# Rotary attention with a spatially gated MLP on one Trainium2 core: the first loads in whole rows, four idle matmuls, and the last store in halves

## The chip, the cores and the metric

The kernel runs on one core of one Trainium2 chip. A core has a matrix engine (TensorE, PE in the profile; its weight loads are listed apart as PEld), a vector engine (VectorE, DVE), a scalar engine (ScalarE, ACT), GpSimd (POOL) and SyncE (SP), which here issues every DMA. [...] The metric is the device time of one execution in microseconds (us), as the median of the runs taken. The profile calls the time between the first and the last instruction the span.

## The reference

Eight batches, eight heads, 576 positions, 64 values per head. Queries and keys are rotated by their position, softmax attention is computed per head, and its output goes through an MLP with a gate that mixes positions:

```python
q_rot, k_rot = rotate(q), rotate(k)              # x1*cos - x2*sin, x1*sin + x2*cos
scores = matmul(q_rot, k_rot.T) / sqrt(64)
attn = exp(scores - max) / (sum(...) + 1e-09)
x = matmul(attn, v)                              # heads side by side: 8 x 576 x 512
h = maximum(x @ w_in, 0);  u, v = halves of h    # 512 wide each
v_n = (v - mean(v)) / sqrt(var(v) + 1e-06)
v_s = einsum('ts,bsd->btd', w_spatial, v_n) + b_spatial[None, :, None]
out = (u * v_s) @ w_out                          # float32, 8 x 576 x 512
```

## The kernel before, in words

Two heads form a pair; there are 32 pairs, four to a batch. For each pair the kernel loads q and k, transposed and laid out as rows of 2 x 576 values (each value, and beside it the partner that the rotation needs), and v. The rotation multiplies a row by a table of cosines and sines (`tabs`) and adds the two halves. For q the table also carries the factor 1/8 (`tabq`, a scaled copy that ACT makes once). Scores are computed in tiles of 128 queries by 576 keys (`sc`, two PSUM buffers): PE multiplies, DVE takes the maximum of each row (`nmx`), ACT takes the exponential (`e`) and sums it. The exponentials are transposed on PE (`tp`), copied out of PSUM (`et` or `eh`) and multiplied by v (`pv`). For the first three pairs q and k are used as plain float32; for the later ones each operand is split into a rounded and a remaining part. The weights of the MLP arrive as 64-bit words and are decoded on DVE and ACT into float32 (`decode`: per 128x512 piece six DVE steps, tiles `dcwi`, `sgwi`, `wi`, `dcwo`, `wo`); this work lies beside the first pairs. Four pairs make a batch; then its MLP runs (`pa` first product and normalisation, `pb` the other half, `pc` mixing of positions, `pd` output), beside the attention of the next batch.

The order on every engine is written out by a small list scheduler at build time (`Program.run`, lines 138 to 220). Each operation is given an engine, an assumed duration, a key, and the names that it reads and writes. The scheduler plays the program through with these assumptions; where an engine is free it takes the ready operation with the lowest key, if a buffer for its result is free. DVE and POOL operations marked `port` are kept apart. On the chip each engine then runs its list strictly in order and waits by semaphores for what it needs. Changing the first operations therefore changes the lists later on as well.

The change touches the work at the very start. In `prepare_whole` (lines 446 to 483) the case `i == 0` handles pair 0: k and the table are loaded in two halves each, alternating (lines 464 and 465), then q (466). DVE multiplies each half of k by its half of the table (469), adds the halves into `kf` (458, 459), multiplies q by the table in two pieces of 192 and 384 columns (473), and adds (474). With `kf` and the first piece of q the first score tile can start (548). In the profile q and k are both named `st`. POOL fills constants in `setup` (290 to 298), first of all the 128x128 identity matrix `ident`, which the transposes use. At the other end, `mlp` stores each output tile `ob` (128x576) with one DMA (806) once ACT has filled both halves (805).

Of the kernel before, what the change touches and what calls it, by code (L numbers as in the profile page):

```python
# [14 lines left out]
ALU = mybir.AluOpType  # L15
AX = mybir.AxisListType
P = 128
# [206 lines left out]
def tile_attention_gated_mlp(  # L224
# [63 lines left out]
        nc.gpsimd.memset(ap.bitcast(F32), value)  # L288

    def setup():  # L290
        make_identity(nc, ident)
        nc.gpsimd.memset(bias, -896.0 * 2**23)
        for t in sums:
            nc.gpsimd.memset(t, 1.0)
        fill(qs[0][:, S:], 0.0)
        fill(qs[1][:, :TW], 0.0)
        fill(qz[64:P, :S], 0.0)
        fill(qz[0:64, S:], 0.0)
# [7 lines left out]
    def load(dst, src):  # L306
        nc.sync.dma_start(out=dst, in_=src)
# [138 lines left out]
    def prepare_whole(i, b, hp, key):  # L446
# [12 lines left out]
            e.tensor_tensor(out=kf[:, :TW], in0=k[:, 4 * P:S], in1=k[:, S + 4 * P:], op=ALU.add)  # L459

        if i == 0:
            for part in range(2):
                cols = slice(S * part, S * part + S)
                op(DMA, 820, -70 + part, lambda part=part, cols=cols: load(k[:, cols], qk[b, hp, 1, :, part]), w=[(k, part)], new=[] if part else [k])
                op(DMA, 820, -70 + part, lambda part=part, cols=cols: load(tabs[:, cols], tab[:, part]), w=[("tabs", part)])
            op(DMA, 1640, -68, lambda: load(q.tile, qk[b, hp, 0].rearrange("p c n -> p (c n)")), w=[q], new=[q])
            op(ACT, 1053, -50, lambda: nc.scalar.activation(tabq, tabs, AF.Copy, scale=0.125), r=[("tabs", 0), ("tabs", 1)], w=["tabq", "tabs"])
            for part in range(2):
                op(DVE, 680, -60, lambda part=part: nc.vector.tensor_tensor(out=turn(k, part, slice(0, S)), in0=turn(k, part, slice(0, S)), in1=turn(tabs, part, slice(0, S)), op=ALU.mult), r=[("tabs", part)], w=[(k, part)], port=True)
            op(DVE, 830, -59, lambda: sum_k(nc.vector), r=[(k, 0), (k, 1)], w=[kf], new=[kf], port=True)  # L470
            for n, (c0, c1) in enumerate(((0, Q0), (Q0, S))):
                cols = slice(c0, c1)
                op(DVE, dve_ns(2 * (c1 - c0)), -58 + 2 * n, lambda cols=cols: nc.vector.scalar_tensor_tensor(out=c2(q.tile)[:, :, cols], in0=c2(q.tile)[:, :, cols], scalar=0.125, in1=c2(tabs)[:, :, cols], op0=ALU.mult, op1=ALU.mult), r=[q, ("tabs", 0), ("tabs", 1)], w=[(q, n)], port=True)
                op(DVE, dve_ns(c1 - c0), -57 + 2 * n, lambda cols=cols: nc.vector.tensor_tensor(out=turn(q, 0, cols), in0=turn(q, 0, cols), in1=turn(q, 1, cols), op=ALU.add), w=[(q, n)], port=True)
# [242 lines left out]
    def mlp(b):  # L717
# [75 lines left out]
        for m in range(4):  # L793
            ob = Buf("m", [P, S], F32, f"ob{b}_{m}")
            for c in range(2):
                pm = Buf(pm_pools, None, None, f"pd{b}_{m}{c}")
                c0 = c * HALF
                for d in range(4):
                    def mul(d=d, m=m, c0=c0, pm=pm):
                        for n, (i, j) in enumerate(((0, 0), (0, 1), (1, 0))):  # L800
                            at = c0 + j * S
                            nc.tensor.matmul(pm[:, :HALF], lhsT=wout[d,][:, i, m * P:(m + 1) * P], rhs=gs[d][:, at:at + HALF], start=(d == 0 and n == 0), stop=(d == 3 and n == 2))  # L802

                    key = mm(3 * pe_ns(HALF), mul, r=[f"wo{d}", (gs[d], 0, c), (gs[d], 1, c)], w=[pm], new=[pm] if d == 0 else [])
                op(ACT, act_ns(HALF), key + K_OB, lambda ob=ob, pm=pm, c0=c0: nc.scalar.activation(ob[:, c0:c0 + HALF], pm[:, :HALF], AF.Copy), r=[pm, *[(ob, 0)][:c]], w=[(ob, c)], new=[ob] if c == 0 else [])
            op(DMA, 800, key + K_OUT, lambda m=m, ob=ob: load(out[b, m * P:(m + 1) * P, :], ob.tile), r=[(ob, 0), (ob, 1)])

    def norm(b, t, pm, key, sum_halves):
# [39 lines left out]

    pairs = [(b, hp) for b in range(B) for hp in range(NP)]
    prepped, xs, chain = [], [], []  # L850
    op(POOL, 800, -26, setup, w=["ident", "bias", ("sums", 0, 0), ("sums", 1, 0), ("qz", 0), ("qz", 1), ("qs", 0, 0), ("qs", 1, 0)])
    prepare(0)
    for c in range(4):
        decode(DEC_V[c], win, (1, c), w_in[c * P:(c + 1) * P, 2 * HF:4 * HF])
# [81 lines left out]
```

## Time and profile before

| what | value |
| --- | --- |
| runs of the kernel before | 967.85, 968.44, 974.62 us; median 968.44 |
| profiled execution | 968.03 us, of which the span is 966.3 us |
| PE busy | 940.3 us, 97% of the span |
| DVE, ACT, POOL busy | 667.7, 734.7, 572.3 us |
| first matmul | 11.04 us after the start of the span |

The views used are the table of busy time by stretch (each engine's busy time in a window, with its number of instructions), the chain of waits (the work that ended last, followed back), the timeline (instructions in order, with the idle time of the engine before them in brackets), the rows of one tile or line (duration of one: smallest, median, largest), the DMA view of a window, and the list of waits. A matmul of float32 operands appears as two instructions in the profile. Neighbouring instructions on an engine can overlap a little, so the distance from one start to the next is at times shorter than a duration.

### The profile page before, as it was taken

The numbers are of one execution on the slowest core, as the hardware profiler recorded it, in microseconds if no ns is written. First come the engines' busy times: TensorE is split into PE (matmuls) and PEld (weight loads), VectorE is DVE, ScalarE is ACT, GpSimd is POOL, SyncE is SP. The second block draws the span as 40 slices with busy tenths as digits, with TensorE's granted clock in tenths as the row PEclk, the third lists the DMA queues.
The fourth block names the chain that finished last, engine by engine and source line by source line (L and its number), as shares of the span: only waits on it lengthen the run. The fifth ranks groups of instructions, "written<-read, shape, count | busy, mean of one in ns | idle before, by whom it ended". The sixth has DMA issues, their size and how long they took to land.

```text
span 966.3 us, 19411 instructions
## 1 busy us (share of the span) xinstructions
PE 940.3 (97%) x6618; PEld 853.8 (88%) x6618; DVE 667.7 (69%) x1484; ACT 734.7 (76%) x1828; POOL 572.3 (59%) x501
## 2 busy tenths in 40 slices
PE   3999999999999999999999999999999999999998
PEld 2455689999899999999899998999889998999998
DVE  5899887766867667666776658676686766866331
ACT  3778788777987779777897779877798678976452
POOL 5851446566757757775666766666586765672121
PEclk9999999999999999999999999999999999999999
DMA  7671743445343553446444444445524455430101
GB/s 280 210 233 27 208 130 109 127 119 152 104 138 110 165 152 84 119 116 180 124 131 114 123 150 124 126 122 151 145 76 130 126 166 145 108 83 13 63 1 50
DMA packets 54581, 121.56 MB, mean 126 GB/s; under 512 B 12881, under 2 KB 12881, under 8 KB 54482
## 3 DMA queue, kind: packets, MB, share of 16 engines
q1 hardware_dynamic: 54482, 120.32, 44.0%
q8 instruction: 53, 0.87, 0.4%
q14 instruction: 46, 0.38, 0.1%
HBM read 66.03 MB, written 9.58 MB: 78 GB/s over the span
## 4 chain that ended last, share of the span: by engine, by line
PE 77%; ACT 9%; DVE 8%; DMA 3%; issue 2%; POOL 0%; SPq 0%; ACTq 0%; DVEq 0%
PE sc L538 12%; PE pc L787 12%; PE pv L602 11%; PE tp L578 11%; PE pd L802 10%; PE pb L769 9%; PE pa L746 5%; ACT e L561 3%; PE sc L548 3%; DVE nmx L559 2%; PE pv L675 2%; ACT eh L589 2%; ACT vv L829 2%; DVE el L313 1%; PE tp L637 1%
## 5 line engine op out<-in xcount | busy, mean ns | idle before, releaser
L589 ACT ACTIVATE eh<-tp 128x384 fp32r<-128x384 f32 (+1 forms) x504 | 217.9, 434 | 84.2 <-PE tp L578 68.5
L313 DVE TENSOR_TENSOR el<-tp,eh 128x384 fp32r<-128x384 f32 x336 | 185.9, 554 | 100.7 <-ACT eh L589 87.0
L559 DVE TENSOR_REDUCE nmx<-sc 128x1 f32<-128x576 f32 x288 | 215.3, 749 | 42.8 <-PE sc L538 34.3
L561 ACT ACTIVATE e<-sc,nmx 128x576 f32<-128x576 f32 x288 | 213.1, 741 | 39.2 <-DVE nmx L559 35.5
L578 PE MATMUL tp<-ident,e 128*128 128x128 f32 (+1 forms) x1176 | 195.6, 273 | 1.8 <-DVE eh L313 0.8
L578 PEld LDWEIGHTS tp<-ident,e 128*128 128x128 f32 (+1 forms) x1176 | 145.2, 138 | 17.0 <-issue 3.7
L602 PE MATMUL pv<-eh,vs 128*128 128x384 f32 (+1 forms) x560 | 154.0, 316 | 0.3 <-ACT x L681 0.2
L402 POOL TENSOR_TENSOR st<-st,tabq 128x576 f32<-128x576 f32 x56 | 79.3, 1432 | 124.8 <-DMA st<-in_qk_dram 109.8
L787 PE MATMUL pc<-wsp,vn 128*128 128x288 f32 x768 | 143.2, 303 | 0.3 <-DVE u L845 0.3
L769 PE MATMUL pb<-x,wi 128*128 128x288 f32 x768 | 142.1, 306 | 0.3 <-ACT u L772 0.3
L802 PE MATMUL pd<-g,wo 128*128 128x288 f32 x768 | 141.2, 303 | 0.0
L746 PE MATMUL pa<-wi,x 128*128 128x512 f32 x448 | 133.3, 407 | 0.0
L538 PE MATMUL sc<-ks,qs 128*128 128x288 f32 x580 | 122.4, 300 | 0.3 <-ACT e L561 0.2
L787 PEld LDWEIGHTS pc<-wsp,vn 128*128 128x128 f32 x768 | 114.9, 189 | 2.6 <-DVE u L845 0.6
L802 PEld LDWEIGHTS pd<-g,wo 128*128 128x128 f32 x768 | 114.2, 189 | 3.3 <-DVE el L313 0.2
L769 PEld LDWEIGHTS pb<-x,wi 128*128 128x128 f32 x768 | 112.0, 189 | 4.0 <-PE pb L769 1.3
L602 PE MATMUL pv<-el,vs 128*64 128x384 f32 (+1 forms) x448 | 113.7, 295 | 0.0
L538 PE MATMUL sc<-lk,qz 128*128 128x288 f32 x522 | 112.0, 296 | 0.0
L712 POOL TENSOR_TENSOR x<-x,rb 128x576 f32<-128x576 f32 x32 | 45.9, 1435 | 110.0 <-DVE x L617 79.9
L602 PEld LDWEIGHTS pv<-eh,vs 128*128 128x128 f32 x560 | 97.7, 188 | 6.1 <-DVE x L617 1.5
L538 PEld LDWEIGHTS sc<-ks,qs 128*128 128x128 f32 x580 | 93.6, 188 | 7.0 <-ACT e L561 1.5
L313 DVE TENSOR_TENSOR eh<-tp,eh 64x256 fp32r<-64x256 f32 (+1 forms) x168 | 59.8, 356 | 48.8 <-ACT eh L589 24.1
(180 smaller groups left out, 1554.7 us busy)
## 6 DMA issues: line engine op xcount, KB each, us to landing
st<-in_qk_dram SPq DMA_DIRECT2D x63, 576.0 KB
ks<-st SPq DMA_DIRECT2D x116, 160.0 KB
qs<-st SPq DMA_DIRECT2D x116, 144.0 KB
vr<-in_v_dram SPq DMA_DIRECT2D x32, 320.0 KB
out_dram<-ob SPq DMA_DIRECT2D x32, 288.0 KB
qz<-st SPq DMA_DIRECT2D x58, 144.0 KB
ws<-in_w_spT_dram SPq DMA_DIRECT2D x2, 576.0 KB
st<-in_qk_dram SPq DMA_DIRECT2D x2, 288.0 KB
```

What stands on the lines that cost most here:

```text
L313: eng.tensor_tensor(out=lo, in0=src, in1=hi.bitcast(F32), op=ALU.subtract)
L402: f = lambda e: e.tensor_tensor(out=st[j][:, cols], in0=st[j][:, cols], in1=(tabs if j else tabq)[:, cols], op=ALU.mult)
L538: nc.tensor.matmul(pt[:, c * 512:c * 512 + HALF], lhsT=lhsT, rhs=rhs[:, k0 + c * HALF:k0 + (c + 1) * HALF], start=(n == 0), stop=(n == len ...
L559: op(DVE, 665, key + K_MAX, lambda: nc.vector.tensor_reduce(out=nmx.tile, in_=tops(), op=ALU.max, axis=AX.XY, negate=True), r=[pt], w=[nmx ...
L561: op(ACT, 730, key + K_EXP, lambda: nc.scalar.activation(e[:, e0:e0 + S].rearrange("p (c n) -> p c n", c=2), tops(), AF.Exp, bias=nmx.tile ...
L578: nc.tensor.transpose(out=tp[:e.shape[1], m * P:m * P + P], in_=e, identity=ident)
L589: nc.scalar.activation(h, p, AF.Copy)
L602: nc.tensor.matmul(pv[0:rows, c1:c2], lhsT=vs[:, kt, h, vp, :], rhs=part[:, c1:c2], start=(kt == 0 and n == 0 and c1 == 0), stop=last)
L746: nc.tensor.matmul(pm.tile, lhsT=lhsT, rhs=win[1, d][:, j, :], start=(d == 0 and n == 0), stop=(d == 3 and n == len(todo) - 1))
L769: nc.tensor.matmul(pm[:, :HALF], lhsT=win[0, d][:, i, f * P:(f + 1) * P], rhs=x[d][:, at:at + HALF], start=(d == 0 and n == 0), stop=(d == ...
L787: nc.tensor.matmul(pm[:, :HALF], lhsT=lhsT, rhs=rhs, start=(t == 0 and n == 0), stop=(t == 4 and n == 1))
L802: nc.tensor.matmul(pm[:, :HALF], lhsT=wout[d,][:, i, m * P:(m + 1) * P], rhs=gs[d][:, at:at + HALF], start=(d == 0 and n == 0), stop=(d == ...
```

## The change

Pair 0 now loads k, then the table, then q, each with one DMA of whole rows. DVE multiplies k by the table in one instruction of 1152 columns, adds, and then finishes the first piece of q (multiply and add) before it begins the second. The identity is made by an operation of its own with an earlier key. Four matmuls of the identity with itself, repeated to 512 columns, are put on PE; nothing reads their result; they use the one PSUM buffer of `pv`. The last output tile of the last batch is stored with two DMAs, one for each half.

```diff
     def setup():
-        make_identity(nc, ident)
         nc.gpsimd.memset(bias, -896.0 * 2**23)
...
         if i == 0:
-            for part in range(2):
-                cols = slice(S * part, S * part + S)
-                op(DMA, 820, -70 + part, lambda part=part, cols=cols: load(k[:, cols], qk[b, hp, 1, :, part]), w=[(k, part)], new=[] if part else [k])
-                op(DMA, 820, -70 + part, lambda part=part, cols=cols: load(tabs[:, cols], tab[:, part]), w=[("tabs", part)])
-            op(DMA, 1640, -68, lambda: load(q.tile, qk[b, hp, 0].rearrange("p c n -> p (c n)")), w=[q], new=[q])
...
-            for part in range(2):
-                op(DVE, 680, -60, lambda part=part: nc.vector.tensor_tensor(out=turn(k, part, slice(0, S)), in0=turn(k, part, slice(0, S)), in1=turn(tabs, part, slice(0, S)), op=ALU.mult), r=[("tabs", part)], w=[(k, part)], port=True)
-            op(DVE, 830, -59, lambda: sum_k(nc.vector), r=[(k, 0), (k, 1)], w=[kf], new=[kf], port=True)
+            whole = lambda t: t.rearrange("p c n -> p (c n)")
+            op(DMA, 1450, -70, lambda: load(k.tile, whole(qk[b, hp, 1])), w=[(k, 0), (k, 1)], new=[k])
+            op(DMA, 1450, -69, lambda: load(tabs, whole(tab)), w=["tabs"])
+            op(DMA, 1450, -68, lambda: load(q.tile, whole(qk[b, hp, 0])), w=[q], new=[q])
...
+            def turn_k():
+                nc.vector.tensor_tensor(out=k[:, :2 * S], in0=k[:, :2 * S], in1=tabs, op=ALU.mult)
+                sum_k(nc.vector)
+
+            def turn_q(cols):
+                both = c2(q.tile)[:, :, cols]
+                nc.vector.scalar_tensor_tensor(out=both, in0=both, scalar=0.125, in1=c2(tabs)[:, :, cols], op0=ALU.mult, op1=ALU.mult)
+                nc.vector.tensor_tensor(out=turn(q, 0, cols), in0=turn(q, 0, cols), in1=turn(q, 1, cols), op=ALU.add)
+
+            op(DVE, 2280, -60, turn_k, r=["tabs"], w=[(k, 0), (k, 1), kf], new=[kf], port=True)
...
+            if (b, m) == (B - 1, 3):
+                for c in range(2):
+                    op(DMA, 400, key + K_OUT, lambda m=m, ob=ob, c0=c * HALF: load(out[b, m * P:(m + 1) * P, c0:c0 + HALF], ob[:, c0:c0 + HALF]), r=[(ob, c)])
+                continue
...
+    op(POOL, 800, -80, lambda: make_identity(nc, ident), w=["ident"])
...
+    for n in range(4):
+        idle = Buf("pv", None, None, f"idle{n}")
+        wide = lambda: ident.rearrange("p (o n) -> p o n", o=1).to_broadcast([P, 4, P])
+        op(PE, 1600, 10000 + n, lambda idle=idle: nc.tensor.matmul(idle.tile.rearrange("p (c n) -> p c n", c=4), lhsT=ident, rhs=wide(), start=True, stop=True), r=["ident"], w=[idle], new=[idle])
```

How the lists move is seen at three places. The first is the start of DVE's list, before (`st_1_94` is k of pair 0, `st_0_103` its q, `st_0_113` the q of pair 1):

```order
L469 TENSOR_TENSOR st_1_94<-st_1_94,tabs 128x576 x2
L458 TENSOR_TENSOR kf_110<-st_1_94 128x576
L459 TENSOR_TENSOR kf_110<-st_1_94 128x64
L473 SCALAR_TENSOR_TENSOR st_0_103<-st_0_103,tabs 128x2x192
L473 SCALAR_TENSOR_TENSOR st_0_103<-st_0_103,tabs 128x2x384
L474 TENSOR_TENSOR st_0_103<-st_0_103 128x192
L474 TENSOR_TENSOR st_0_103<-st_0_103 128x384
L480 TENSOR_TENSOR st_0_113<-st_0_113,tabq 128x576
L559 TENSOR_REDUCE nmx_0_0_130<-sc_0_0_121 128x1
```

and the same place in the changed kernel (`st_1_87`, `st_0_105`, `st_0_116` are the same three):

```order
L468 TENSOR_TENSOR st_1_87<-st_1_87,tabs 128x1152
L457 TENSOR_TENSOR kf_112<-st_1_87 128x576
L458 TENSOR_TENSOR kf_112<-st_1_87 128x64
L473 SCALAR_TENSOR_TENSOR st_0_105<-st_0_105,tabs 128x2x192
L474 TENSOR_TENSOR st_0_105<-st_0_105 128x192
L473 SCALAR_TENSOR_TENSOR st_0_105<-st_0_105,tabs 128x2x384
L474 TENSOR_TENSOR st_0_105<-st_0_105 128x384
L484 TENSOR_TENSOR st_0_116<-st_0_116,tabq 128x576
L563 TENSOR_REDUCE nmx_0_0_137<-sc_0_0_126 128x1
```

One multiplication of 1152 columns stands for two of 576, and the add of q's first piece has moved ahead of the multiplication of the second piece. The work ahead of the first maximum is otherwise the same.

The second place is DVE's list from the second maximum to the fifth, before:

```order
L559 TENSOR_REDUCE nmx_1_0_137<-sc_1_0_127 128x1
L480 TENSOR_TENSOR st_1_117<-st_1_117,tabs 128x576
L559 TENSOR_REDUCE nmx_0_1_150<-sc_0_1_141 128x1
L559 TENSOR_REDUCE nmx_1_1_155<-sc_1_1_147 128x1
L458 TENSOR_TENSOR kf_159<-st_1_117 128x576
L459 TENSOR_TENSOR kf_159<-st_1_117 128x64
L480 TENSOR_TENSOR st_0_133<-st_0_133,tabq 128x576 x2
L559 TENSOR_REDUCE nmx_0_2_175<-sc_0_2_165 128x1
```

and in the changed kernel:

```order
L563 TENSOR_REDUCE nmx_1_0_140<-sc_1_0_132 128x1
L484 TENSOR_TENSOR st_1_122<-st_1_122,tabs 128x576 x2
L485 TENSOR_TENSOR st_0_116<-st_0_116 128x576
L563 TENSOR_REDUCE nmx_0_1_158<-sc_0_1_148 128x1
L563 TENSOR_REDUCE nmx_1_1_163<-sc_1_1_153 128x1
L484 TENSOR_TENSOR st_0_135<-st_0_135,tabq 128x576 x2
L344 TENSOR_SCALAR dcwi_180<-wi10raw 128x512
L563 TENSOR_REDUCE nmx_0_2_183<-sc_0_2_171 128x1
```

DVE now does both multiplications of pair 1's k and the add of its q, and the adds into pair 1's `kf` have gone to POOL. Between the first and the last (ninth) maximum of pair 0 stand seven decoding steps before and after; of other work four multiplications or adds of 576 columns and the two adds into `kf` before, and five of 576 columns after.

The third place is PE's list, whose beginning is now (before, it began with the first `sc` row):

```order
L864 MATMUL idle_96<-ident 128x512
L864 MATMUL idle_103<-ident 128x512
L864 MATMUL idle_109<-ident 128x512
L864 MATMUL idle_118<-ident 128x512
L552 MATMUL sc_0_0_126<-kf_112,st_0_105 128x288 x2
L552 MATMUL sc_1_0_132<-kf_112,st_0_105 128x288 x2
```

The four idle matmuls stand ahead of the first scores in the queue. Each waits for the one before it, and the first for `ident` from POOL. POOL's own list begins as before, since the identity was its first work already. Further on, single operations of the first pairs and the first MLP have changed places in the lists of all engines; after about a sixth of PE's list (some 600 of its rows) and a fifth of DVE's the lists name the same work row for row, but for the two last stores.

## Rows read from the trace of the kernel before

**Rows 1.** Busy time by stretch: the window in us and its length, then busy us and number of instructions of PE, PEld, DVE, ACT and POOL, the granted clock of PE (1.00 is full), the share of the DMA engines and what they moved.

```profile
8.00:32.00 24.00, 16.62 (x51) 9.54 (x53) 19.48 (x31) 10.82 (x25) 13.20 (x9) 1.00 0.82 318
32.00:64.00 32.00, 31.63 (x173) 16.50 (x171) 28.52 (x51) 25.60 (x62) 25.25 (x24) 1.00 0.71 207
64.00:112.00 48.00, 44.34 (x280) 27.11 (x276) 44.21 (x76) 37.73 (x91) 15.84 (x16) 1.00 0.40 117
...
130.00:962.00 832.00, 829.61 (x6009) 787.04 (x6008) 559.86 (x1297) 644.28 (x1616) 508.06 (x433) 1.00 0.42 115
```

**Rows 2.** The chain of waits through the start: start in us, length in us, what.

```profile
2.12 5.48 DMA tabs<-in_tab_dram
...
7.70 0.77 DVE st L469
8.49 0.76 DVE kf L458
9.25 0.14 DVE kf L459
9.39 1.34 DVE st L473 x2
10.72 0.28 DVE st L474
11.04 2.30 PE sc L548 x8
13.37 0.77 DVE nmx L559
...
51.97 1.12 PE sc L548 x8
```

**Rows 3.** The timeline of DVE and of some PE work: start, busy us, engine, line, operation, count, and in brackets the idle time before it and what ended it.

```profile
4.51 0.76 DVE L469 TENSOR_TENSOR st<-st,tabs 128x576 f32<-128x576 f32 x1 [4.51 <-DMA tabs<-in_tab_dram]
...
11.48 0.76 DVE L480 TENSOR_TENSOR st<-st,tabq 128x576 f32<-128x576 f32 x1
...
13.37 1.42 DVE L559 TENSOR_REDUCE nmx<-sc 128x1 f32<-128x576 f32 x2 [1.12 <-PE sc L548]
...
15.11 3.01 PE L548 MATMUL sc<-kf,st 64*128 64x288 f32 x8 [1.76 <-ACT e L561]
...
17.43 1.55 DVE L559 TENSOR_REDUCE nmx<-sc 128x1 f32<-128x576 f32 x2 [1.96 <-PE sc L548]
18.89 1.17 DVE L458 TENSOR_TENSOR kf<-st 128x576 f32<-128x576 f32 x1
20.12 1.42 DVE L480 TENSOR_TENSOR st<-st,tabq 128x576 f32<-128x576 f32 x2
21.50 1.54 DVE L559 TENSOR_REDUCE nmx<-sc 128x1 f32<-128x576 f32 x2
...
23.18 3.07 PE L548 MATMUL sc<-kf,st 64*128 64x288 f32 x8 [1.00 <-ACT e L561]
...
25.57 1.54 DVE L559 TENSOR_REDUCE nmx<-sc 128x1 f32<-128x576 f32 x2 [0.67 <-PE sc L548]
...
27.66 0.90 PE L637 MATMUL tp_0b<-ident,e 128*128 128x128 f32 x3 [0.58 <-ACT et_0a L644]
...
30.72 0.76 DVE L559 TENSOR_REDUCE nmx<-sc 128x1 f32<-128x576 f32 x1 [0.63 <-PE sc L548]
66.44 1.23 PE L548 MATMUL sc<-kf,st 64*128 64x288 f32 x4 [0.90 <-ACT e L561]
```

**Rows 4.** Busy time in the stretch from the first to the end of the last maximum of pair 0 (columns as in Rows 1).

```profile
13.37:31.48 18.11, 13.80 (x43) 8.09 (x43) 14.77 (x23) 9.50 (x22) 10.87 (x9) 1.00 0.76 286
```

**Rows 5.** Durations in ns of one instruction (smallest, median, largest): the DVE operations of pair 0's rotation, from the rows of the tile `st`, and then the matmuls of line 548 between 11 and 32 us, and between 32.5 and 62 us.

```profile
L469 DVE TENSOR_TENSOR st<-st,tabs x2: 758/758/759, 4.5 to 7.7; 128x576 f32<-128x576 f32 x2
L473 DVE SCALAR_TENSOR_TENSOR st<-st,tabs x2: 551/752/952, 9.3 to 9.8; 128x384 f32<-128x384 f32 x1, 128x768 f32<-128x768 f32 x1
L474 DVE TENSOR_TENSOR st<-st x2: 351/452/552, 10.6 to 10.9; 128x192 f32<-128x192 f32 x1, 128x384 f32<-128x384 f32 x1
...
L548 PE MATMUL sc<-kf,st x40: 681/684/847, 11.0 to 30.0; 64*128 64x288 f32 x32, 64*64 64x288 f32 x8
...
L548 PE MATMUL sc<-kf,st x48: 402/403/507, 33.0 to 58.1; 64*128 64x288 f32 x40, 64*64 64x288 f32 x8
```

**Rows 6.** What the DMA queue moved in four windows of 2 us: 0 to 2, 2 to 4, 4 to 6 and 8 to 10 us.

```profile
DMA packets 14, 0.03 MB, mean 16 GB/s; under 512 B 0, under 2 KB 0, under 8 KB 14
...
DMA packets 296, 0.61 MB, mean 306 GB/s; under 512 B 30, under 2 KB 30, under 8 KB 296
...
DMA packets 251, 0.55 MB, mean 274 GB/s; under 512 B 28, under 2 KB 28, under 8 KB 251
...
DMA packets 233, 0.85 MB, mean 424 GB/s; under 512 B 25, under 2 KB 25, under 8 KB 233
```

**Rows 7.** The waits of PE between 32 and 130 us: who waited for whom, us in total, times, the longest.

```profile
PE sc L548 <- ACT e L561: 0.9, 1, 0.9
PE tp_1a L637 <- ACT et_0b L644: 0.7, 1, 0.7
PE tp_2a L637 <- DVE et_1b L646: 0.7, 1, 0.7
PE tp L637 <- ACT et_3b L644: 0.6, 1, 0.6
PE tp_3a L637 <- ACT et_2b L644: 0.6, 1, 0.6
```

**Rows 8.** The end: the last two evacuations and the last store in the timeline, and what the DMA engines moved between 950 and 970 us, in 40 slices of 0.5 us.

```profile
962.43 0.75 ACT L805 ACTIVATE ob<-pd 128x288 f32<-128x288 f32 x2 [2.49 <-PE pd L802]
963.21 0.33 SPq L307 DMA_DIRECT2D out_dram<-ob  x1
...
GB/s 0 0 0 0 0 0 0 0 134 410 46 0 0 0 0 360 226 0 0 9 18 166 387 46 0 0 0 0 355 235 0 0 0 0 0 0 0 0 0 0
```

**Rows 9.** The first instructions of POOL that make the identity, and the first of SP, in the timeline.

```profile
1.02 0.29 POOL masks.py:199 TENSOR_SCALAR_AFFINE_SELECT ident<-ident 128x128 f32<-128x128 f32 x1
1.18 0.42 SPq L307 DMA_DIRECT2D tabs<-in_tab_dram  x1
2.12 0.43 SPq L307 DMA_DIRECT2D tabs<-in_tab_dram  x1
```

More of the change, by code (lines that the diff above doesn't have):

```diff
@@ L467, in prepare_whole @@
-            op(ACT, 1053, -50, lambda: nc.scalar.activation(tabq, tabs, AF.Copy, scale=0.125), r=[("tabs", 0), ("tabs", 1)], w=["tabq", "tabs"])
-            for part in range(2):
-                op(DVE, 680, -60, lambda part=part: nc.vector.tensor_tensor(out=turn(k, part, slice(0, S)), in0=turn(k, part, slice(0, S)), in1=turn(tabs, part, slice(0, S)), op=ALU.mult), r=[("tabs", part)], w=[(k, part)], port=True)
-            op(DVE, 830, -59, lambda: sum_k(nc.vector), r=[(k, 0), (k, 1)], w=[kf], new=[kf], port=True)
+            whole = lambda t: t.rearrange("p c n -> p (c n)")
@@ new lines, in prepare_whole @@
+            op(DMA, 1450, -70, lambda: load(k.tile, whole(qk[b, hp, 1])), w=[(k, 0), (k, 1)], new=[k])
+            op(DMA, 1450, -69, lambda: load(tabs, whole(tab)), w=["tabs"])
+            op(DMA, 1450, -68, lambda: load(q.tile, whole(qk[b, hp, 0])), w=[q], new=[q])
+            op(ACT, 1053, -50, lambda: nc.scalar.activation(tabq, tabs, AF.Copy, scale=0.125), r=["tabs"], w=["tabq"])
+            def turn_k():
+                nc.vector.tensor_tensor(out=k[:, :2 * S], in0=k[:, :2 * S], in1=tabs, op=ALU.mult)
+                sum_k(nc.vector)
@@ L471, in prepare_whole @@
+            def turn_q(cols):
[3 more added lines that the diff above has]
+            op(DVE, 2280, -60, turn_k, r=["tabs"], w=[(k, 0), (k, 1), kf], new=[kf], port=True)
             for n, (c0, c1) in enumerate(((0, Q0), (Q0, S))):
-                cols = slice(c0, c1)
@@ L473, in prepare_whole @@
-                op(DVE, dve_ns(2 * (c1 - c0)), -58 + 2 * n, lambda cols=cols: nc.vector.scalar_tensor_tensor(out=c2(q.tile)[:, :, cols], in0=c2(q.tile)[:, :, cols], scalar=0.125, in1=c2(tabs)[:, :, cols], op0=ALU.mult, op1=ALU.mult), r=[q, ("tabs", 0), ("tabs", 1)], w=[(q, n)], port=True)
-                op(DVE, dve_ns(c1 - c0), -57 + 2 * n, lambda cols=cols: nc.vector.tensor_tensor(out=turn(q, 0, cols), in0=turn(q, 0, cols), in1=turn(q, 1, cols), op=ALU.add), w=[(q, n)], port=True)
+                op(DVE, dve_ns(2 * (c1 - c0)) + dve_ns(c1 - c0), -58 + 2 * n, lambda c0=c0, c1=c1: turn_q(slice(c0, c1)), r=[q, "tabs"], w=[(q, n)], port=True)
@@ L850, in tile_attention_gated_mlp @@
     prepped, xs, chain = [], [], []
-    op(POOL, 800, -26, setup, w=["ident", "bias", ("sums", 0, 0), ("sums", 1, 0), ("qz", 0), ("qz", 1), ("qs", 0, 0), ("qs", 1, 0)])
+    op(POOL, 800, -80, lambda: make_identity(nc, ident), w=["ident"])
+    op(POOL, 800, -26, setup, w=["bias", ("sums", 0, 0), ("sums", 1, 0), ("qz", 0), ("qz", 1), ("qs", 0, 0), ("qs", 1, 0)])
+    for n in range(4):
+        idle = Buf("pv", None, None, f"idle{n}")
+        wide = lambda: ident.rearrange("p (o n) -> p o n", o=1).to_broadcast([P, 4, P])
+        op(PE, 1600, 10000 + n, lambda idle=idle: nc.tensor.matmul(idle.tile.rearrange("p (c n) -> p c n", c=4), lhsT=ident, rhs=wide(), start=True, stop=True), r=["ident"], w=[idle], new=[idle])
     prepare(0)
```

## The prediction

> **What bounds the kernel now.** I read the busy time by stretch first, because an average over the span hides that the kernel has two parts [rows 1]. From 130 us to the end of the matmuls PE is busy for 829.61 of 832.00 us, and from 32 to 64 us for 31.63 of 32. There PE does one thing after another, so work that reaches it some microseconds earlier ends that much earlier, and the gain is kept to the end. The exceptions are the first 32 us and the stretch from 64 to 112 us, where PE stands for 48.00 - 44.34 = 3.66 us while DVE is busy for 44.21 of 48 us. Since the lists name the same work after about a sixth of PE's list, the question is how many microseconds the start gives, and whether the stretch with the full DVE takes them back.
>
> Then the chain of waits shows what the start consists of [rows 2]. The table's second half is the last input: DVE waits for it until 7.70 us. From there DVE alone is on the chain: half of k, the adds, q, until PE starts at 11.04. Next comes a cycle of PE, DVE and ACT: scores, maximum, exponential, and the exponential frees the PSUM buffer for the next scores. The timeline gives its length: pairs of maxima start at 13.37, 17.43, 21.50 and 25.57 us, so 4.07 us per pair of tiles, and DVE stands before each first maximum except one, 1.12, 1.96 and 0.67 us, for PE [rows 3].
>
> Last, the speed of PE. The granted clock reads 1.00 in every stretch [rows 1], so this column does not show the difference; the durations do. The same eight score instructions took 2.30 us at 11.04 and 1.12 us at 51.97 [rows 2], and one of them has a median of 684 ns before 32 us and 403 ns after [rows 5]. [...] PE paused between the score pairs all through the first part, and at 66.44 it paused for 0.90 us at the higher level and still took 1.23 us for four instructions [rows 3].
>
> **The change, part by part.** *Loads.* k and the table are 2 x 128 x 1152 x 4 bytes = 1.18 MB, before as after; q follows them in both lists. In halves, with rows of 2304 bytes, the queue moved 0.61 MB from 2 to 4 us and 0.55 MB from 4 to 6 us; where rows of 4608 bytes are the bulk, 0.85 MB from 8 to 10 us, 424 GB/s [rows 6]. At this rate 1.15 MB after the first 0.03 take 2.7 us, to 4.7 us. DVE got its data later than the sum of bytes says: the first halves (0.59 MB, moved by about 3.9 us) at 4.51 [rows 3], all four (1.19 MB by 6.0 us) at 7.70 [rows 2], a lag of 0.6 and 1.7 us. So the table lands at 5.3 to 6.4 us. I take 6.0, nearer the larger lag, since there too later loads were already queued. The other end is 7.70, the old rate. The table's issue also moves from 2.12 to about 1.18, with no half of k ahead of it [rows 9].
>
> *DVE ahead of the scores.* A multiplication of 576 columns takes 758 ns, and an operation of 192 columns 351 ns, so 1.06 ns a column; 1152 columns are an estimate of 0.758 + 576 x 0.00106 = 1.37 us [rows 5]. The adds for k are 9.39 - 8.49 = 0.90 us; q's first piece is 1.34 - 0.95 = 0.39 us, and its add with the step to PE 11.04 - 10.72 = 0.32 us [rows 2, 5]. The first score can start 1.37 + 0.90 + 0.39 + 0.32 = 3.0 us after the table, at 9.0 instead of 11.04. The first maximum is later, because DVE has the rest of q and one multiplication of pair 1 ahead of it: from 8.49 to 11.48 + 0.76 = 12.24 this was 3.75 us [rows 2, 3], with 1.37 it is 5.1 us, so 11.1 us. **Term one: 13.37 - 11.1 = 2.3 us.** In this count the second half of the multiplication of k is no longer hidden behind its load; that is in the 1.37.
>
> *Idle matmuls.* The identity is there at 1.31 us [rows 9], and PE has nothing else until 9.0. Their price is bounded by the score pairs: one piece of 288 columns takes 2.30 / 2 = 1.15 us at the lower level and 1.12 / 2 = 0.56 at the higher [rows 2]; 512 columns are then 2.0 or 1.0 us, four are 8.2 or 4.0 us. They end between 5.5 and 9.7 us; with half of them at each level at about 7.6. So they cost nothing, covered by the 7.6 us in which PE has no input; at the worst they hold the first score back by 0.7 us. What they may bring is the higher level for the scores, 1.1 us less per pair of tiles.
>
> *The score cycle.* From the first maximum to the end of the ninth it is 18.11 us, of which DVE is busy for 14.77 [rows 4]. With PE at the higher level the cycle would be 4.07 - 1.15 = 2.9 us, and DVE's list becomes the limit: between two pairs of maxima it now has 3.5 to 3.8 us of work. Its sum is 14.77 less the two adds into `kf` that went to POOL (20.12 - 18.89 = 1.23), less 0.09 of the next instruction, plus one more operation of 576 columns (1.42 / 2 = 0.71): 14.2 us [rows 3, 4]. No wait at all would be a gain of 3.9; from 32 to 64 us, at the higher level, DVE is busy 28.52 / 32 = 89% [rows 1], which makes 14.2 / 0.89 = 15.9 us. I take that as the nearest row. **Term two: 18.1 - 15.9 = 2.2 us**, with bounds of 3.9 and 0.9 (below). The adds into `kf` cost POOL nothing that counts: POOL is busy for 13.20 of 24 us there [rows 1].
>
> *The last store.* It is issued at 963.21, its bytes move until 965.0, and the span ends at 966.3 [rows 8]. The first half can go one evacuation (0.75 / 2 = 0.37 us) earlier, and then its 147 KB are gone before the second half comes; a store's 0.29 MB take about 0.8 us. **Term three: 0.35 us**, bounds 0 (two issues of 0.33 us behind each other) and 0.4.
>
> *Between 64 and 112 us* I put nothing: PE's waits there are 0.6 to 0.9 us each [rows 7], and a new order of the same work moves them both ways. Bounds: a gain of 3.66 if they all went, and a loss in the rivals.
>
> **Sum:** 2.3 + 2.2 + 0.35 = 4.85 us from the profiled execution's 968.03, which gives 963.2. This execution lies 0.4 below the median of 968.44, so I forecast 963.6.
>
> **Rivals.** *The higher level is not kept (or not reached).* The idle matmuls end before the scores, then PE works little more than 1.2 us in each 3.7, with pauses longer than the 0.90 us that did no harm at 66.44 [rows 3]. For it: all through the first part PE paused for 1.0 to 1.8 us between the pairs and stayed at the lower level [rows 3]. Against: it came to those pauses from the lower level, and no row shows a fall from the higher. Price: the pairs again take 4.07 us, and only one group of transposes (0.90 us) leaves the way to the ninth maximum [rows 3], so term two is 0.9; the first maximum waits for a slow score until 9.0 + 2.3 = 11.3, or 12.0 with the overrun. Term one is 2.0 or 1.3. That gives 968.44 - 3.2 to 2.6, about 965.5. [...]
>
> *The table comes no earlier.* If the lag, not the rate, sets 7.70, the first maximum comes at 12.8 and term one is 0.6: 965.3. For it: the lag grew from 0.6 to 1.7 us as the queue filled. Against: whole rows moved 1.4 to 1.5 times as fast.
>
> *DVE takes it back, and more: slower than before.* In the stretch from 64 to 112 us DVE has only 3.8 us free, and with an earlier start the decoded weights are wanted earlier by the same work. If ten evacuations or exponentials there each wait for one more DVE instruction of 0.75 us, PE loses 7.5 us: 963.6 + 7.5 = 971. It ends above the old time once PE's standing there grows by more than 4.85 us, from 3.66 to over 8.5. Against: only five waits of PE are listed in all that time [rows 7], most of them for ACT.
>
> *Everything goes well.* Table at 5.3 (3.0), DVE without a wait (3.9), the five waits gone (3.5), 0.35 from the store: 957.7.
>
> **How the numbers follow.** Chances: the forecast 0.48, level not kept 0.22, table no earlier 0.12, slower 0.10, everything well 0.08. The time is the forecast's, 963.6. The range from 959.5 to 968.0 holds the first three cases with the bounds of their terms and half of the last; it leaves out the slower case and the other half, with the tails about 0.2. One per cent, about what a measurement of this kernel can tell from no change, is 9.7 us: 958.8 to 978.1. Only the best case gets below (0.04), and only a slower case twice as bad as the one I worked out gets above (0.03); 0.93 is left for within.
>
> **What would show it.** The table's wait should end near 6.0 us, the first score start near 9.0 and the first maximum near 11.1. The four idle matmuls should show 2.0 us each at first and 1.0 later; the first score pair should take 1.2 us, and median score instructions 403 ns, not 684. The pairs of maxima should be 3.5 to 3.9 us apart with DVE nearly full; the ninth should end near 27 us instead of 31.5. From 32 us on, equal work should come 4 to 5 us earlier. I am wrong if PE's score instructions are at 684 ns again after the idle ones, if the table lands after 7 us, or if PE's standing time between 60 and 110 us is far from 3.66 us.

## The result, and the profile after

The changed kernel is slower: 974.21 us in the median of 20 runs (972.20 to 978.41), against 968.80 us for 20 runs of the kernel before on the same chip. The ratio is 1.006, with a 95% interval from 1.0047 to 1.0073. The forecast was 963.6 us, with a range to 968.0. The profiled execution took 976.07 us with a span of 974.2, that is 7.9 us more than the span before. Its mean granted clock is 0.984; of the 20 runs, eleven with 0.989 to 0.991 took 972.2 to 974.4 us and nine with 0.982 to 0.986, the profiled one among them, 975.2 to 978.4. The profile below is thus one of the slower nine.

The busy time by stretch of the kernel after, with the columns of [rows 1]:

```profile
8.00:32.00 24.00, 15.51 (x49) 9.29 (x50) 21.62 (x30) 10.91 (x26) 14.33 (x12) 0.58 0.81 309
32.00:64.00 32.00, 31.20 (x146) 16.21 (x145) 25.36 (x45) 21.58 (x51) 19.78 (x17) 0.84 0.59 181
64.00:112.00 48.00, 44.08 (x264) 24.83 (x261) 43.97 (x75) 36.68 (x89) 13.88 (x14) 1.00 0.29 88
112.00:130.00 18.00, 15.65 (x106) 11.55 (x105) 13.55 (x22) 13.61 (x35) 8.18 (x6) 1.00 0.66 187
...
26.60:41.90 15.30, 15.13 (x46) 7.32 (x45) 9.04 (x16) 8.14 (x18) 10.65 (x10) 0.50 0.44 136
42.20:42.40 0.20, 0.20 (x2) 0.06 (x2) 0.20 (x1) 0.00 (x0) 0.20 (x1) 0.50 0.50 205
42.40:43.00 0.60, 0.60 (x5) 0.03 (x1) 0.60 (x2) 0.00 (x0) 0.60 (x1) 0.97 0.22 75
```

Read the clock column first. Between 32 and 64 us it is 0.84, where it was 1.00 [rows 1]. PE is at 0.50 until 42.4 us, although from 26.6 on it is busy for 15.13 of 15.30 us. In that stretch PE is busy and slow: 146 matmuls instead of 173 in the same 32 us. I call 0.50 the lower level: a score instruction has a median of 684 ns there (from 14.4 to 42 us), and 402 ns at the higher level (from 44.9 to 62 us). The forecast's lower and higher level are the same two speeds, 684 and 403 ns before [rows 5]. From 64 to 112 us PE stands for 3.92 us, hardly more than the 3.66 before.

The start in the timeline, with the columns of [rows 3]: DVE, then PE, then POOL.

```profile
6.29 1.36 DVE L468 TENSOR_TENSOR st<-st,tabs 128x1152 f32<-128x1152 f32 x1 [6.29 <-DMA tabs<-in_tab_dram]
...
10.34 0.56 DVE L474 TENSOR_TENSOR st<-st 128x384 f32<-128x384 f32 x1
10.82 1.95 DVE L484 TENSOR_TENSOR st<-st,tabq 128x576 f32<-128x576 f32 x1
12.69 1.41 DVE L563 TENSOR_REDUCE nmx<-sc 128x1 f32<-128x576 f32 x2
16.74 1.55 DVE L563 TENSOR_REDUCE nmx<-sc 128x1 f32<-128x576 f32 x2 [0.64 <-PE sc L552]
...
29.89 0.76 DVE L563 TENSOR_REDUCE nmx<-sc 128x1 f32<-128x576 f32 x1 [0.70 <-PE sc L552]
```

```profile
1.37 6.29 PE L864 MATMUL idle<-ident 128*128 128x512 f32 x8 [1.37 <-POOL ident masks.py:199]
9.49 1.25 PE L552 MATMUL sc<-kf,st 64*128 64x288 f32 x8 [1.83 <-DVE st L474]
14.42 3.01 PE L552 MATMUL sc<-kf,st 64*128 64x288 f32 x8 [3.68 <-ACT e L565]
```

```profile
10.42 1.73 POOL L484 TENSOR_TENSOR st<-st,tabq 128x576 f32<-128x576 f32 x1 [5.34 <-DMA st<-in_qk_dram]
```

The new loads work: the table is waited for until 6.29 us instead of 7.70 [rows 2], and the first score starts at 9.49 instead of 11.04. It takes 1.25 us for the work that took 2.30, so PE was at its higher level. The next score takes 3.01 us, as before: after a pause of 3.68 us PE is at the lower level again. The column falls within that pause, from 1.00 up to 11.7 us to 0.50 from 11.8 us on. The first maximum starts only 0.68 us earlier than before (12.69 against 13.37), because DVE's line 484 took 1.95 us where the same operation took 0.76 [rows 3]. POOL's own multiplication had started 0.40 us before it; it took 1.73 us, and DVE's add of 10.34 was still running when it began. In the kernel before DVE's started first, at 11.48 [rows 3], and then POOL's was the long one, 1942 ns for 1396; one line's instructions there, with durations in ns (smallest, median, largest) and first and last start:

```profile
L480 POOL TENSOR_TENSOR st<-st,tabs x3: 1394/1396/1396, 13.5 to 18.0; 128x576 f32<-128x576 f32 x3
...
L480 POOL TENSOR_TENSOR st<-st,tabq x1: 1942/1942/1942, 11.6 to 11.6; 128x576 f32<-128x576 f32 x1
```

The waits of PE between 32 and 130 us, columns as in [rows 7]:

```profile
PE sc L542 <- ACT e L565: 2.2, 3, 1.2
PE pa L750 <- DVE el L312: 1.6, 1, 1.6
PE tp L641 <- ACT et L648: 1.0, 2, 0.6
PE tp L641 <- DVE wi L312: 0.7, 1, 0.7
```

These are not the waits of [rows 7]: pair 3's scores now wait for exponentials, and a group of the MLP's first product (`pa`) waits 1.6 us for `el`. That is the remaining part of a group of exponentials, which DVE takes out of PSUM (tile `tp`). In kernel.py `tp` and `pa` share one pool of PSUM buffers, so the product probably waits for a buffer; the row does not say it. The chain of waits (columns as in [rows 2]) tells what is late there:

```profile
91.10 1.20 DVE dcwo L344 x2
92.30 0.52 DVE nmx L563
92.94 0.69 DVE dcwo L352
93.63 0.66 DVE nmx L563
94.29 0.52 DVE dcwo L353
94.85 0.76 DVE nmx L563
95.61 0.45 DVE sgwo L350
```

DVE's list puts steps of the weights' decoding between the maxima, and in this chain exponentials and scores wait behind them. Such steps stand between maxima in the kernel before as well, so the chain shows where PE waits and not by itself what the new order did.

**One account for all kernels.** From 32 us on PE is busy nearly all the time, so the change of a span can be split into three parts. The first is PE's standing from 32 us to the end. The second is an estimate of the time lost to the lower level: a window's length times one minus its granted clock, from windows of 4 us up to the last matmuls. It takes work at 0.50 to go half as fast; by the score instructions, 402 ns for 684, the loss would be 0.41 of a window and not 0.50. What is left over is what the start gave. The first comes from these two rows of the kernel before and two of the kernel after:

```profile
32.00:130.00 98.00, 93.34 (x559) 56.70 (x556) 87.30 (x158) 77.23 (x188) 46.83 (x44) 1.00 0.55 159
130.00:966.30 836.30, 830.35 (x6013) 787.54 (x6011) 559.86 (x1297) 645.03 (x1618) 508.06 (x433) 1.00 0.42 115
```

```profile
32.00:130.00 98.00, 90.93 (x510) 52.59 (x510) 82.88 (x140) 71.86 (x174) 41.84 (x36) 0.95 0.46 136
130.00:974.20 844.20, 838.26 (x6061) 795.10 (x6060) 567.14 (x1313) 650.35 (x1630) 510.77 (x436) 1.00 0.42 117
```

Before, PE stands for 4.66 + 5.95 = 10.61 us; after, for 7.07 + 5.94 = 13.01, so 2.40 more. By the estimate the clock costs 5.20 us between 32 and 44 us. Together 7.6 of the 7.9 us; in this execution the account leaves nothing for the start. The same sum for each kernel below, in us (growth of standing and span against before):

| kernel | median, ratio (95%) | span | standing | clock | start's remainder |
|---|---|---|---|---|---|
| after | 974.21, 1.0060 (1.0047-1.0073) | +7.9 | +2.4 | 5.2 | -0.3 |
| no idle matmuls | 975.75, 1.0098 (1.0085-1.0111) | +7.3 | +2.9 | 5.1 | 0.8 |
| idle matmuls alone | 967.58, 0.9999 (0.9982-1.0016) | -0.4 | -0.2 | 0.0 | 0.2 |
| more idle, new order | 970.48, 1.0035 (1.0012-1.0059) | -0.9 | +2.6 | 0.0 | 3.5 |
| new loads, old order | 967.83, 1.0002 (0.9991-1.0014) | -0.3 | +0.5 | 0.0 | 0.8 |
| old loads, new order | 974.48, 1.0071 (1.0055-1.0086) | +4.0 | +2.7 | 1.7 | 0.4 |
| whole change, old order | 967.61, 1.0000 (0.9991-1.0008) | -0.5 | 0.0 | 0.4 | 0.9 |
| the same, more idle | 969.43, 1.0015 (1.0002-1.0028) | +2.2 | 0.0 | 6.8 | 4.6 |
| the same, idle in pair 1 too | 967.61, 0.9983 (0.9965-1.0001) | +0.1 | +1.0 | 1.7 | 2.6 |
| before, second order | 970.87, 1.0017 (0.9997-1.0037) | +4.8 | +3.3 | 3.2 | 1.7 |
| before, third order | 970.78, 1.0013 (0.9991-1.0035) | +1.2 | +2.4 | 0.0 | 1.2 |

The spans are of one execution each; the ratios are of all runs. The remainder is not a measurement of its own: where the order is the old one, the end of pair 0 (the start of DVE's reciprocal of its sums of exponentials) shows the lead directly (0.5, 1.0, 0.3, 3.6 and 3.8 us, in the order of the table), and the remainder misses it by up to 1.2 us. The clock of the second order is worked out with that run, since the column does not show all of it.

### The profile page after: what moved, and what is told of

The parts are those of the page before. It is cut to its first block, busy times and chain, and to the rows that moved or that the text cites. A ratio compares the mean times of both kernels' runs of the same rounds, so it can differ in the third digit from the quotient of the medians.

```text
span 974.2 us, 19427 instructions
## 1 busy us (share of the span) xinstructions
PE 950.8 (98%) x6626; PEld 858.6 (88%) x6626; DVE 673.3 (69%) x1483; ACT 735.6 (76%) x1830; POOL 571.2 (59%) x499
## 4 chain that ended last, share of the span: by engine, by line
PE 76%; ACT 11%; DVE 9%; issue 2%; DMA 1%; SPq 0%; ACTq 0%; DVEq 0%
PE pc L791 12%; PE sc L542 12%; PE pv L606 11%; PE tp L582 11%; PE pd L806 11%; PE pb L773 9%; PE pa L750 5%; ACT e L565 3%; DVE nmx L563 3%; PE sc L552 3%; ACT eh L593 2%; ACT vv L837 2%; PE pv L679 2%; DVE el L312 1%; ACT avt L623 1%
## 5 line engine op out<-in xcount | busy, mean ns | idle before, releaser
L312 POOL TENSOR_TENSOR g<-u,g 128x288 fp32r<-128x288 f32 x64 | 51.8, 816 | 69.2 <-ACT g L309 63.1
```

The costliest lines, as they stand in the source:

```text
L312: eng.tensor_tensor(out=lo, in0=src, in1=hi.bitcast(F32), op=ALU.subtract)
```

## The experiments

My first theory was that the idle matmuls did harm: PE falls from the higher level after them and comes back late.

**Without the idle matmuls.** All other places in all lists stay as in the changed kernel.

```diff
-    for n in range(4):
-        idle = Buf("pv", None, None, f"idle{n}")
...
```

> The changed kernel without its four idle matmuls; every other list is the same. Theory one (the clock): the idle matmuls raise PE's level early, it is lost again at 11.7 us in the pauses between the score pairs, and PE then stays at the lower level until about 42 us, where before it left it at 32; without them no such fall, the higher level comes near 30 us, and the time is 964 to 967 us, faster than before. Rival (the order): what costs is the new order on DVE, where two multiplications ran beside POOL at 1.95 and 1.64 us instead of 0.75; then this kernel stays at 972 to 974. Third: the new order of PE's own work keeps the level low until 42 us with or without idle matmuls; then 972 to 974 too, but score instructions stay at 684 ns until about 42 us in the trace.

It took 975.75 us, a little more than with them. PE gets through 23 matmuls from 32 to 36 us, where the changed kernel, at 0.50, gets through 13. But the column falls again at 49.9 us (0.95 from 49 to 50, 0.50 from 50 to 51), and once more between 92 and 96 us, where it reads 0.78:

```profile
48.00:52.00 4.00, 3.97 (x17) 2.02 (x15) 3.77 (x7) 1.85 (x4) 1.40 (x1) 0.74 0.96 298
52.00:56.00 4.00, 4.00 (x22) 2.60 (x22) 1.98 (x5) 2.26 (x7) 1.41 (x1) 0.50 0.60 241
```

The theory fell: it had 964 to 967 us. The idle matmuls do not make the change slow.

**The idle matmuls alone**, in the kernel before, with all other places as before.

```diff
+    for n in range(4):
+        idle = Buf("pv", None, None, f"idle{n}")
...
```

> The kernel before with only the four idle matmuls put in; every other list is the kernel's before. Theory one (the clock): the level is raised near 5 us, lost before the scores have gone through, and regained later than 32 us; the time is 971 to 976 us. Rivals (the order on DVE, or of PE's work): the idle matmuls end before the first score and the time stays at 968 to 969.5.

It took 967.58 us, and the run beside it of the kernel before 967.81. The first score pair takes 1.94 us from 10.76 on, between the 1.25 and the 2.30 of the two levels; so the level falls in it, as an estimate from these three at about 11.2 us. The column reads 0.50 up to 31.6 us and 0.93 in the 0.4 us behind it: no gain and no loss.

**More idle matmuls between the score pairs**, in the changed kernel, so that PE does not pause there.

```diff
+            if (i, a) == (0, 1) and t < 4:
+                for _ in range(2):
+                    fill_pe(idles[-1])
```

> The changed kernel with two more idle matmuls behind each of the first four score pairs, otherwise the same lists. Theory one (the clock): PE's pauses shrink to under 2 us, the level of 5 us is kept, score instructions stay at about 400 ns, and the time is 960 to 965 us. Rival (the order on DVE): PE's level is not what limits, the time stays at 971 to 974, or grows where the idle matmuls stand ahead of a score.

It took 970.48 us, between the two forecasts. Its profiled execution is the fastest of nine, 967.16 us. There the clock is 1.00 from 12 us on, and by the account the start gives 3.5 us, near what terms one and two promised together (4.5). Three more runs with a mean clock of 1.00 took 969.87 to 970.05, so executions differ by 3 us without the clock.

```profile
12.00:32.00 20.00, 18.23 (x78) 9.54 (x78) 18.90 (x31) 12.77 (x30) 16.15 (x14) 1.00 0.78 291
32.00:130.00 98.00, 90.77 (x540) 55.71 (x537) 86.52 (x154) 75.71 (x186) 39.85 (x35) 1.00 0.53 156
```

But PE stands for 98.00 - 90.77 = 7.23 us between 32 and 130 us, as in the changed kernel, and its longest waits are nearly the same:

```profile
PE sc L542 <- ACT e L568: 2.2, 3, 1.2
PE pa L753 <- DVE el L312: 1.3, 1, 1.3
```

So the standing does not come from the clock. What these kernels share is the order in the lists.

**New loads, old order.** The work of the change without the idle matmuls; the scheduler's assumed durations are set so that every other operation stands where it stood before.

```diff
-            op(DVE, 2280, -60, turn_k, r=["tabs"], w=[(k, 0), (k, 1), kf], new=[kf], port=True)
+            op(DVE, 1628, -60, turn_k, r=["tabs"], w=[(k, 0), (k, 1), kf], new=[kf], port=True)
...
```

> The changed loads, DVE pieces and last store, without idle matmuls, but with the assumed durations of the four operations at the start set so that the scheduler gives every other operation its place of before. Theory one (the order): the loss comes from where the scheduler puts the work of pairs 1 to 3 once the start is planned differently; with the places of before the earlier start is kept, the first score starts near 9.4 us, and the time is 965 to 967 us. Rival (the loads themselves, that is what the earlier start collides with): 972 to 976 as in the run without idle matmuls.

It took 967.83 us, as the kernel before, where 965 to 967 had been expected. This kernel and the one without idle matmuls do the same work. PE has the same 6618 instructions in both, and ACT has 1828 for 1830, POOL 501 for 499. These counts hide exchanges, for the scheduler may also choose the engine of some operations. By the tiles of the two traces, at least six operations on two tensors went from DVE to POOL in the new order and eight from POOL to DVE, and six copies from DVE to ACT and four back. The order and this choice differ together, and the times are 7.9 us apart. What is called the order here holds both; no run separates them.

Its pair 0 ends 1.0 us ahead of before and keeps that lead until 439 us. Then one wait, at 454 us, takes most of it, and before has none between 430 and 475 us:

```profile
PE tp L582 <- DVE eh L312: 0.7, 1, 0.7
```

**Old loads, new order.** The order of the run without idle matmuls, with k and the table loaded and multiplied in halves as before.

```diff
+            def load_half(p):
+                load(half(k, p), qk[b, hp, 1, :, p])
+                load(half(tabs, p), tab[:, p])
...
```

> The order of the changed kernel without idle matmuls, but with k and the table loaded and multiplied in halves as before. Theory one (the order): the loss is there without the new loads, and the start is 1 to 2 us later; 975 to 979 us. Rival (the loads themselves): 967 to 969 us.

It took 974.48 us, a little below the 975 to 979 expected; the profiled execution, 972.40, is the fastest of six. With the loads of before and the order of after, the time is that of after.

**The whole change, old order**: idle matmuls, new loads, halved store, each other operation where it was.

> All that the change names (whole rows, four idle matmuls, halves of the last store) at the places of before. Theory one (the order): as the run without idle matmuls at these places, 964 to 967 us, because the level is lost again in the first pauses. If the fall of the level is what costs, 968 us or more.

It took 967.61 us, above the 964 to 967 expected. This and the changed kernel again do the same work, with 6626 instructions on PE, and are 6.6 us apart (5.5 if each is taken against the runs of before beside it). The clock is back within 0.44 us lost after 32 us, where the changed kernel loses 5.20. What the idle matmuls and the halved store bring together is too little to measure.

**The same, with two more idle matmuls behind each of three score pairs.**

> The new loads at the places of before, with the four idle matmuls and two more behind each of the first three score pairs. Theory one (the order): level kept from 5 us on, first maximum near 12 us, cycle of 3.3 to 3.7 us instead of 4.07, and PE's waits from 32 to 130 us at 4 to 5 us as before: 961 to 965 us. Rival (a faster start is always used up by DVE's full stretch between 64 and 112 us): PE's waits there grow to over 7 us and the time is 966 to 970.

It took 969.43 us, where 961 to 965 had been expected. Pair 0 ends at 30.59 instead of 34.20 us, and the lead is lost here:

```profile
60.00:64.00 4.00, 3.10 (x18) 1.76 (x18) 4.00 (x8) 4.00 (x10) 3.85 (x4) 1.00 0.90 252
64.00:68.00 4.00, 4.00 (x15) 2.12 (x14) 4.00 (x7) 2.88 (x9) 0.89 (x1) 0.71 0.39 159
68.00:72.00 4.00, 4.00 (x12) 1.96 (x11) 2.68 (x5) 1.90 (x5) 0.00 (x0) 0.50 0.00 0
```

PE stands for 0.90 us, and then its level falls and, by the estimate, 6.8 us are lost. The rival has the right time but the wrong cause: PE stands for 5.11 us from 32 to 130 us, not for over 7. In the kernel before the same scores waited for 0.90 us too [rows 3], and the level stayed.

**Idle products behind pair 1's values as well**, where that pause lies. They go into columns of `pv` that nothing reads.

```diff
+                if (i, c, kt) == (1, 0, 4):
+                    for _ in range(4):
+                        nc.tensor.matmul(pv[:, 384:512], lhsT=ident, rhs=ident, start=True, stop=True)
```

> As the run with the old order, four idle matmuls and two behind each of three score pairs, and now four idle products of 128 columns into spare columns behind pair 1's last values, where PE stood for 0.90 us at 62.5 us and the granted clock fell from 65 to 79 us. Theory A (span = start's lead, PE's standing and the granted clock, and nothing else): if the level holds, the first pair ends 3.6 us ahead of before and stays so, span 962.5 to 964, time 964.3 to 965.8, ratio 0.996 to 0.998. If the level falls elsewhere, time lost to it comes back one for one. Theory B (a lead at the start is lost later, to DVE or to waits, whatever the clock does): span 966 or more with the clock at 1.00 all through.

It took 967.61 us against 968.13; the interval reaches 1.0001, so it can't be told from before, though it is below the changed kernel. The level now holds from 64 to 80 us, but PE waits 2.62 us at 34.84 and the level falls there:

```profile
34.84 0.90 PE L644 MATMUL tp_2b<-ident,e 128*128 128x128 f32 x3 [2.62 <-ACT et_2a L651]
```

```profile
32.00:36.00 4.00, 1.38 (x8) 1.14 (x6) 1.21 (x3) 1.85 (x4) 2.37 (x3) 0.86 0.30 76
36.00:40.00 4.00, 4.00 (x17) 1.56 (x16) 3.25 (x6) 3.06 (x7) 4.00 (x4) 0.72 0.46 109
```

One of its runs shows a mean clock of 1.00; it took 964.51 us, inside what was expected for a level that holds. That is one run; the other eleven, at 0.996 to 0.998, took 964.9 to 970.1.

**Other orders of the kernel before.** One assumed duration is changed; the work stays.

```diff
-            op(DMA, 1640, -68, lambda: load(q.tile, qk[b, hp, 0].rearrange("p c n -> p (c n)")), w=[q], new=[q])
+            op(DMA, 1450, -68, lambda: load(q.tile, qk[b, hp, 0].rearrange("p c n -> p (c n)")), w=[q], new=[q])
```

> The kernel before with one number changed that no instruction carries: q's first load is assumed to take 1450 ns instead of 1640. Loads, multiplications, matmuls and stores are those of before, the scheduler writes them in another order (246 places of PE's list differ). Theory A (an order by itself costs some us, and the old one was a good draw): PE's standing between 32 and 130 us leaves the 4.65 us of before by over 1 us, or the granted clock falls once after 32 us, and the span moves by just these two amounts, 968 to 974 us against 966.3; the ratio of the times is 1.002 to 1.008. Theory B (the loss belongs to the order that the change's own work brought, and other orders are as good as the old): within 0.1% of before, 967 to 969 us.

The second is k's two multiplications, 1300 for 680:

> The kernel before with the assumed time of k's two multiplications at 1300 instead of 680 ns, again with no other edit; a third order, of those found nearest to the order of after (146 places of PE's list differ from it, 238 from it to before). Theory A: span 966.3 plus the growth of PE's standing between 32 and 130 us plus the time lost to the granted clock after 32 us, 968 to 974 us, whatever the two amounts are. Theory B: within 0.1% of before unless its pair 3 scores wait for ACT as in after; then 2 to 3 us slower.

They took 970.87 and 970.78 us against 968.13. Both intervals hold 1, so the times show neither to be slower. Of the 29 runs of before beside them, nine have a mean clock of 0.992 or 0.993 and took 972.0 to 973.7 us, which widens the intervals; the other twenty took 966.4 to 970.3. The second order's twelve, none below 0.997, took 968.8 to 974.9. This was compared only afterwards; it suggests that the second order is slower. The spans of the profiled executions grow by 4.8 and 1.2 us, and the first is found in PE's row:

```profile
32.00:130.00 98.00, 90.02 (x524) 52.99 (x525) 84.43 (x144) 72.78 (x176) 43.76 (x38) 0.98 0.49 144
```

PE stands for 7.98 us between 32 and 130 us instead of 4.66. An order alone moves PE's standing by more than the whole change did.

The orders also differ in when PE first reaches the higher level. The granted clock reads 1.00 there in all three, but the transposes show it: 0.90 us each group at the lower level, 0.55 at the higher. The second order, the kernel before and the third order:

```profile
34.19 0.90 PE L637 MATMUL tp_1b<-ident,e 128*128 128x128 f32 x3
36.61 0.55 PE L637 MATMUL tp_2b<-ident,e 128*128 128x128 f32 x3
```

```profile
30.60 0.90 PE L637 MATMUL tp_1a<-ident,e 128*128 128x128 f32 x3
32.55 0.55 PE L637 MATMUL tp_1b<-ident,e 128*128 128x128 f32 x3
```

```profile
28.84 0.67 PE L637 MATMUL tp_0b<-ident,e 128*128 128x128 f32 x3
30.60 0.55 PE L637 MATMUL tp_1a<-ident,e 128*128 128x128 f32 x3
```

That is about 35, 32 and 29 us. For the second order 3 us more at the lower level are an estimate of 1.5 us, taken at the 0.50 that the column reads for this level in the changed kernel; here the column does not show them. With the 1.7 us that it does show, they make 3.2 us. The sum is then 966.3 + 3.3 + 3.2 = 972.8 and the span 971.1, a miss of 1.7 us. For the third order the sum from 32 us on gives 968.7 and the span is 967.5, a miss of 1.2 us; by the same estimate its earlier return is worth 1.5.

**What is shown and what stays open.** Twice the same work in two orders was 6.6 and 7.9 us apart, and the loads of before in the new order were as slow as the change. So the order, with the choice of engines that comes with it, costs the time. The account, good to between one and two us, puts it into PE's standing and the lower level for one profiled execution of each kernel.

It does not hold in this form for every run. Eleven of the changed kernel's twenty runs have the mean clock, 0.989 to 0.991, of all runs of the idle matmuls alone and of the whole change in the old order, whose profiles lose at most 0.44 us to the level after 32 us. Yet these eleven took 972.2 to 974.4 us, and the others 966.9 to 969.7 and 966.1 to 968.6. So most of the order's price is paid in runs with no more of the lower level than those two kernels have: by the medians 972.7 against 967.6 us, 5 of the 6.6. What it consists of there, no trace shows. The late return to 42.4 us belongs to the slower nine as far as the mean clocks tell.

Open is also which place of the order sets the level. No run has the kernel before with idle matmuls between its score pairs; the nearest has the new loads. In the changed kernel it returned at 42.4 us and in the whole change with the old order at 32.8, though the last pause of PE that the timeline lists ahead of it came at 27.66 us in the one (0.17 us) and at 26.64 in the other (0.58).

## Why the prediction was wrong

The step that failed is the sentence that put the stretch after the start at zero, together with the one it rests on, that "a new order of the same work moves them both ways". I looked for a loss only in PE's waits from 64 to 112 us, and there it is small: 3.92 us against 3.66. But the new lists reach from 12 to 130 us. What they cost lies ahead of and behind that stretch: in the profiled execution an estimated 5.2 us of lower level from 32 to 42.4 us, and 18.00 - 15.65 = 2.35 us of standing from 112 to 130, of which 1.6 is the one wait for `el`. In the kernel before PE stood for 0.63 us there:

```profile
112.00:130.00 18.00, 17.37 (x112) 13.10 (x111) 14.57 (x33) 13.89 (x37) 5.73 (x6) 1.00 0.68 188
```

That the gain of the start "is kept to the end" does not hold either: with the new loads in the old order a lead of 1.0 us was gone behind one wait at 454 us.

*Loads:* right. 6.29 us for 6.0 forecast. *DVE ahead of the scores:* half right. The multiplication took 1.36 us for 1.37, and the first score came at 9.49 for 9.0. The first maximum came at 12.69 for 11.1, since I priced the multiplication of pair 1 at its 0.76 us, and now POOL's came first; that is 1.2 of the 1.6 us. The new order is not the reason: with the new loads in the old order the same operation took 1.95 us too, from 10.71. **Term one** measured 0.7 us instead of 2.3. In these rows whichever of the two came second was the long one: 1.95 us for 0.76 on DVE, begun 0.40 us after POOL's; 1.94 for 1.40 on POOL in the kernel before, begun 0.08 us after DVE's. POOL's 1.73 began during DVE's add. What held the later one, no trace shows.

*Idle matmuls:* right in their cost, which is nothing, and in the first score at the higher level; they end at 7.66 us for 7.6 forecast. No row had shown when the level would rise, so that this came out so close is partly luck: of their eight instructions those begun by 3.5 us took 1061 to 1222 ns, the one begun at 4.5 took 781, and those begun from 5.4 on 592 to 697. *Score cycle:* **term two** failed as the first rival said, since the level fell at 11.7 us and the pairs took 3.01 us again. From the first maximum to the end of the ninth it is 30.65 - 12.69 = 17.96 us, 0.15 less than before, not 2.2. The rival's price, 965.5 us, was wrong: its terms one and two were 1.3 to 2.0 and 0.9 and measured 0.7 and 0.15, and I counted the lower level up to the ninth maximum and no further, while in the profiled execution it lasted to 42.4. PE did fall between the scores, but the estimated 5.2 us from 32 us on lie in work nearly without pauses.

*The last store:* **term three** was 0.2 for 0.35. From the end of the last evacuations to the end of the span it is 974.2 - 971.28 = 2.92 us, before 966.3 - 963.18 = 3.12 [rows 8].

*The slower rival* had the right sign and the right kind of cause (DVE's list), at the wrong place and with too small a chance of 0.10. It had DVE take the time back from 64 to 112 us. The range ended at 968.0, below the time of before. The waits that spoke against it (I counted five [rows 7]; the view lists three more, of 0.2 us each) belonged to the old order; they were no bound for a new one, with DVE busy for 44.21 of 48 us [rows 1].

## What to carry to other kernels

Where a scheduler writes the lists from assumed durations, a change at the start is two changes: the work, and another order for everything after it. Separate them first: set the assumed durations so that the old order comes out with the new work, and only then judge the work. Here that showed a change worth nothing where the plain comparison showed one that costs 0.6%. When a level of TensorE's clock is in question, price it through to where the rows show it back, in busy stretches as well as in pauses.

## What was not expected of the hardware

- In the profiled execution of the changed kernel PE stayed at 0.50 from 11.8 to 42.4 us, the last 15 us of it in work nearly without a gap. From 32 us on the account puts this at 5.2 us, in a busy stretch.
- The same work in three orders first reached the higher level at about 29, 32 and 35 us.
- The same wait of 0.90 us for the same scores was followed by a fall of the level in one kernel and not in another. A pause's length alone did not decide it here.
- In the kernel before, the column of the granted clock reads 1.00 in the first 32 us while score instructions take 684 ns, against 403 ns later [rows 1, 5]. In the kernels with idle matmuls it reads 0.50 for such instructions. So in that trace 1.00 at the start does not show the higher level; the durations do.
